# Pass one of a gated layer: the next tile's input products ahead of the output products, and four smaller moves

## The chip, the cores and the metric

One core of a Trainium2 chip runs the kernel. The metric is the device time of one execution in microseconds (us), the median of three runs. The engines are TensorE (PE, with PEld for its weight loads), VectorE (DVE), ScalarE (ACT), GpSimd (POOL) and SyncE (SP), which issues nearly all DMAs.

## The reference

Banded local attention and global attention (4 batches, 8 heads, 512 local and 32 global tokens each, 2176 tokens in all) give `x` with 512 features. `x` goes through two layers:

```
gated:     y = (sigmoid(x @ w_gate) * (x @ w_val)) @ w_out          # 512 -> 1536 -> 512
rational:  h = y @ w_in;   out = (P(h) / Q(h)) @ w_out2             # 512 -> 2048 -> 512, P and Q polynomials
```

The weights come as 64-bit floats and the result has to keep more precision than one 32-bit product gives.

## The kernel before

**Precision.** Each weight block is loaded raw and *converted* on the chip into a high and a low part in the matmul's 32-bit format (names ending in gv, in, out: the gate/value weights, the rational layer's first weights, and either layer's output weights). One conversion is a chain over three engines: two ACT operations (L566, L567), three on DVE (L574 to L576), an addition on POOL (L583), a high part on ACT (L605), a low part on POOL (L613), for some blocks further sums (combine: DVE L631, L634, L636, POOL L632, L643, ACT L642), and a store through SP (L597, from tiles named `st..` to DRAM tensors named `k..`). A product of two split operands is three matmuls (high by high, low by high, high by low), so twelve for the 512 features of one 128x512 output.

**Tiles.** The tokens lie in five tiles, 0 to 3 of 512 tokens and GLOB (4) of 128. The inner features `f` of the gated layer are 12 blocks of 128, and go in pairs `f0`, `f0+1`.

**Pass one** (the loop at L919 to L959) does tiles 0, 1 and GLOB for six pairs, f0 = 0, 2, .., 10. Its pieces:

- `first(f, i)`: 12 matmuls into `pg`, 12 into `pv` (L713 to L715), then the gate: sigmoid on ACT (L751), product on DVE (L752), high part on ACT (L759, `gh`), low part on DVE (L764, `gl`).
- `first_glob(f0)`: the same for GLOB with the operands turned; it ends with the gate product `t_glob` on DVE (L752).
- `turn(f0, t)`: PE transposes `t_glob` (L789, tile `pt`), then the split `gh_glob` (ACT L759) and `gl_glob` (DVE L764).
- `second_glob(f0, gg)`: six matmuls with `gh_glob` and `gl_glob` (L797 to L799), added to `gacc` on DVE (L806).
- halves (`second`, made by `pair_of`): 12 matmuls of output products each (L831 to L833), two additions to `gacc` on DVE (L845). A pair's two halves for one tile are kept in `pending` and placed later; in the last pair the sums are also split for DRAM (L848, L849), and `parks` holds such splits.

The order of an iteration before the change is: first(f0, 0), the two halves of tile 1 from the pair before, first(f0+1, 0), first_glob, the two halves of tile 0, turn, first(f0, 1), first(f0+1, 1), second_glob. Between the pieces `spot` lets `Pace` issue conversion steps, so that their instructions stand in the engines' queues among the others.

**Pass two** does tiles 2 and 3 for the other pairs by a Strassen scheme (`strassen`, L972, called for f = 2 to 11), in which sums `w`, `u`, `s` of PSUM results (L994) stand between products, with a list `fill` of halves placed between them, and `pace = Pace(actions, 143.0)` spreads the remaining conversions. `back(i)` (L964) asks tile i's results back from DRAM, eight SP DMAs (L969, L970); `rest()` (L1111) places the last halves.

**The rational layer** (`rational`, L1119) follows a table of operations per 128x512 unit. On ACT it makes `u`, `v` and `t1` (L1152, L1155, L1163), on POOL a product (L1159) and the low part `rgl` (L1213), on PE the output products (L1242 to L1244). `new` (L1136) takes the buffers: `t1` from the pool `rest`, which lies where the gated layer's closed pool was, with the stage tiles `st..` of the last conversions.

All engines run their instructions in program order, and SP its DMAs; nothing is reordered at run time. PSUM gives three banks to `ps1` (`pg`, `pv`) and five to `ps2`.

Of the kernel before, what the change touches and what calls it, by code (L numbers as in the profile page):

```python
# [8 lines left out]
F32 = mybir.dt.float32  # L9
# [699 lines left out]
def layer(nc, ps, wp, net, f, i, mh, ml):  # L709

    for k in range(4):
        wh, wl = wp.block(net, f, i, k)
        nc.tensor.matmul(ps, wh, mh[:, k], start=k == 0, stop=False)  # L713
        nc.tensor.matmul(ps, wh, ml[:, k], start=False, stop=False)  # L714
        nc.tensor.matmul(ps, wl, mh[:, k], start=False, stop=k == 3)  # L715
# [20 lines left out]
def gated(nc, pools, only, xpool, dram, wp, ident, xh, xl):  # L736
    G = G1
    NF = FF // 128
    L = 2.72
# [8 lines left out]
    def gate(pg, pv, name):  # L748

        t = pools.t.tile([128, 512], F32, tag="u", name=f"t{name}")[:, 0 : pg.shape[1]]  # L750
        nc.scalar.activation(t, pg, AF.Sigmoid)  # L751
        nc.vector.tensor_tensor(t, pv, t, ALU.mult)  # L752
        return t
# [12 lines left out]
    def split(t, name):  # L766
        g = high(t, name)
        low(t, g)
        return g

    def first(f, i):
        pg = pools.ps1.tile([128, 512], F32, tag="p1", name=f"pg{f}_{i}")
        pv = pools.ps1.tile([128, 512], F32, tag="p1", name=f"pv{f}_{i}")
        layer(nc, pg, wp, 1, f, "gate", xh[i], xl[i])
        layer(nc, pv, wp, 1, f, "val", xh[i], xl[i])
        return split(gate(pg, pv, f"{f}_{i}"), f"{f}_{i}")
# [43 lines left out]
    parks = []  # L820
# [52 lines left out]
    def ztile(name):  # L873
        return only.tile([128, 512], F32, tag="z", name=name, bufs=5)
# [11 lines left out]
    def less(dst, x, y, eng):  # L886

        for d, a, b in zip(dst, x, y):
            eng.tensor_tensor(d, a, b, ALU.subtract)
        eng.tensor_tensor(dst[0], dst[0], dst[1], ALU.add)  # L890

    def at(rc, k):
        return [t[:, k] for t in part[rc]]
# [18 lines left out]
    def c3(k):  # L912
        held["d", k], held["e", k] = ztile(f"zd{k}"), ztile(f"ze{k}")
        less((held["d", k], held["e", k]), at((1, 1), k), at((0, 1), k), nc.gpsimd)
# [4 lines left out]
    for p, f0 in enumerate(range(0, NF, G)):  # L919
        pace = Pace(wp.plan[p], 34.0)  # L920
        extra = {}
        if f0 + G == NF:
            load = lambda: wp.allow(1)
            extra = {0: [load], 1: [load], 2: [lambda: c1(0)], 3: [load], 4: [load, lambda: c2(0)], 5: [load, lambda: c4(0)],
                     6: [load], 7: [lambda: c3(0)] + [lambda: parks.pop(0)()] * 2, 8: [lambda: parks.pop(0)()] * 2}
        spots = iter(range(9))

        def spot(dt):
            pace.advance(dt)
            for step in extra.get(next(spots), []):  # L930
                step()

        gs = [first(f0, 0)]
        if p == 0:
            for step, j in wp.urgent[6:]:
                step(j)
        spot(2 * L)
        for half in pending or [lambda: None] * 2:
            half()
            spot(L if pending else 0)  # L940
        gs.append(first(f0 + 1, 0))
        pending = pair_of(f0, 0, gs)
        spot(2 * L)
        t = first_glob(f0)
        spot(3)
        for half in pending:
            half()
            spot(L)
        gg = turn(f0, t)
        gs = [first(f0, 1)]  # L950
        spot(2 * L)
        gs.append(first(f0 + 1, 1))
        second_glob(f0, gg)
        pending = pair_of(f0, 1, gs)
        for g in range(G):
            for h in range(2):
                wp.release((1, f0 + g, "gv", h))
        spot(0)
        pace.finish()  # L959
# [3 lines left out]
    actions = list(wp.plan[-1])  # L963
    def back(i):  # L964
        yh[i] = xpool.tile([128, 4, 512], F32R, tag=f"xh{i}", name=f"yh{i}")
        yl[i] = xpool.tile([128, 4, 512], F32R, tag=f"xl{i}", name=f"yl{i}")
        for m in range(4):
            t = wp.kept[9, i, "y", m]
            nc.sync.dma_start(yh[i][:, m].bitcast(F32), t[:, 0:512])  # L969
            nc.sync.dma_start(yl[i][:, m].bitcast(F32), t[:, 512:1024])  # L970

    def strassen(f, fill, before, gs):  # L972
        x = {(r, c): (xh[2 + c][:, 2 * r : 2 * r + 2], xl[2 + c][:, 2 * r : 2 * r + 2]) for r in range(2) for c in range(2)}
        def product(ps, key, moving, start):
            t = wp.have[1, f, key, 0]
            mh, ml = moving
            for k in range(2):
                w, v = slice(k * 128, k * 128 + 128), slice(256 + k * 128, 384 + k * 128)
                nc.tensor.matmul(ps, t[:, w], mh[:, k], start=start and k == 0, stop=False, skip_group_check=True)
                nc.tensor.matmul(ps, t[:, w], ml[:, k], start=False, stop=False, skip_group_check=True)  # L980
                nc.tensor.matmul(ps, t[:, v], mh[:, k], start=False, stop=k == 1, skip_group_check=True)

        def done(key):
            wp.release((1, f, key, 0))
            wp.pump(len(wp.loads))

        def bank(name):
            return pools.ps1.tile([128, 512], F32, tag="p1", name=f"{name}{f}")

        def tile(name):  # L990
            return only.tile([128, 512], F32, tag="z", name=f"{name}{f}", bufs=5)

        def add(out, ps, t):
            nc.vector.tensor_tensor(out, ps, t, ALU.add)  # L994

        def late(n):
            if before:
                before[n]()

        a, b, c = bank("pa"), bank("pb"), bank("pc")  # L1000
        product(a, "g0", x[0, 0], True)
        s1 = tile("s")
        nc.scalar.copy(s1, a)
        late(0)
        product(b, "s2", turned[1], True)
        done("g0")
        u2 = tile("u")
        add(u2, b, s1)
        late(1)
        product(c, "s1", turned[0], True)  # L1010
        late(2)
        if f == NF - 1:
            back(0)
        product(a, "g1", x[1, 0], False)
        done("s1")
        t0 = pools.t.tile([128, 512], F32, tag="u", name=f"t{f}_2")
        nc.scalar.activation(t0, a, AF.Sigmoid)
        late(3)
        pace.advance(2 * L)
        for half in fill[0:1]:  # L1020
            half()
            pace.advance(L)
        product(b, "s3", turned[2], False)
        u3 = tile("w")
        add(u3, b, s1)
        add(u3, c, u3)
        pace.advance(L / 2)
        for half in fill[1:2]:
            half()
            pace.advance(L)  # L1030
        product(b, "v1", turned[3], False)
        if f == NF - 1:
            back(1)
        done("s3")
        add(s1, b, s1)
        product(c, "s4", x[1, 1], False)
        done("s4")
        add(u2, c, u2)
        pace.advance(L)
        g = {}  # L1040

        def l0():
            nc.gpsimd.tensor_tensor(t0, s1, t0, ALU.mult)
            nc.scalar.activation(u2, u2, AF.Sigmoid)

        def l1():
            gs[0].append(g0 := high(t0, f"{f}_2"))
            g[0] = g0
            nc.gpsimd.tensor_tensor(u2, u3, u2, ALU.mult)

        def l2():
            low(t0, g[0])

        def l3():
            gs[1].append(g1 := high(u2, f"{f}_3"))
            low(u2, g1, nc.gpsimd)

        return [l0, l1, l2, l3]
# [5 lines left out]
    gs = [first(0, 2)]  # L1064
# [17 lines left out]
    gs = [first(0, 3)]  # L1082
# [13 lines left out]
        for h in range(2):  # L1096
            wp.release((1, f, "gv", h))
    wp.allow(len(wp.loads))
    pace = Pace(actions, 143.0)
    queue, tail = pair_of(0, 3, gs), []  # L1100
    for f0 in range(G, NF, G):
        sets, per = ([], []), len(queue) // G
        for f in range(f0, f0 + G):
            tail = strassen(f, queue[0:per], tail, sets)
            queue = queue[per:]
        queue = pair_of(f0, 2, sets[0]) + pair_of(f0, 3, sets[1])
# [4 lines left out]
    def rest():  # L1111
        for _ in range(2):
            queue.pop(0)()
        wp.pump(len(wp.loads))

    return yh, yl, rest
# [2 lines left out]
def rational(nc, pools, rest, wp, ident, xh, xl, before, co, out):  # L1119
    G = G2  # L1120
    NF = FF2 // 128
# [12 lines left out]
    st = [dict() for _ in units]  # L1134

    def new(u, name):  # L1136
        pool = {"u": pools.t, "v": wp.early}.get(name, rest)
        t = st[u][name] = pool.tile([128, 512], F32, tag=name, name=f"{name}{u}", bufs=3)
        return t

    def first(u):

        fs, i = units[u]
        ps = st[u]["h"] = pools.ps1.tile([128, 512], F32, tag="p1", name=f"rp{u}")
        if i == GLOB:
            turned_layer(nc, ps, wp, 2, fs[0], xh[i], xl[i])
        else:
            layer(nc, ps, wp, 2, fs[0], "in", xh[i], xl[i])
# [124 lines left out]
    for n in range(len(units) + 8):  # L1273
        for name, ahead, *args in PLAN2:
            u = n + ahead
# [117 lines left out]
```

## Time and profile before

| | |
|---|---|
| three runs | 956.99, 956.1, 956.0 us; median 956.1 |
| profiled execution | 957.4 us, span 955.6 us, granted clock 0.982 |
| busy share of the span | PE 95%, PEld 79%, DVE 79%, ACT 61%, POOL 60% |
| chain that ended last | PE 69%, POOL 9%, DVE 9%, issue 5%, DMA 4%, ACT 2% |
| attention | 0 to 125 us |
| pass one | 143 to 368 us |
| pass two | 401 to 552 us |
| rational layer | 555 us to the end |

A timeline row gives the start in us from the span's start, the duration in us, engine, line, operation and tiles, and in brackets the engine's idle time just before with what ended it. A matmul's duration there is its passage through the array: the next one starts 0.22 to 0.23 us later. A count (x4) joins equal instructions that follow one another.

### The profile page before, as it was taken

Reading aid. Unit: us, or ns where it says so; the run is one execution under the profiler, and the core shown is the slowest. Engines: PE = TensorE matmul, PEld = TensorE weight load, DVE = VectorE, ACT = ScalarE, POOL = GpSimd, SP = SyncE. Lnnn points to the kernel's source line nnn. Section 1 sums busy time; section 2 is a strip of 40 time slices with the busy share of each in tenths; the row PEclk is TensorE's granted clock in tenths of the full one; section 3 lists DMA queues with packets and bytes.
Section 4 is the critical chain, followed back from the end, with each engine's and each line's share of the span. In section 5 each row is a group of like instructions: output and inputs, shape, how many; then the busy total and the mean of one; then the engine's idle time right before and its main releaser. Section 6 shows DMA issues by size and latency. Waiting matters only on the chain.

```text
span 955.6 us, 13762 instructions
## 1 busy us (share of the span) xinstructions
PE 910.9 (95%) x4666; PEld 750.5 (79%) x4666; DVE 753.0 (79%) x1355; ACT 580.9 (61%) x1161; POOL 572.5 (60%) x470
## 2 busy tenths in 40 slices
PE   8989999898989899989999977999999999999998
PEld 6768888687867778868888856888888888888886
DVE  6988885887878777866866738977788899888887
ACT  6978963554545444343344436777776778777773
POOL 4765865666666755444666635544465667566564
PEclk9999999899999999999999998999999999999999
DMA  9865264666667677688888971003200310020112
GB/s 303 242 200 146 79 244 176 238 242 229 246 212 253 218 276 266 234 281 291 293 296 282 339 273 45 1 1 105 72 1 1 110 67 1 1 89 1 45 55 88
DMA packets 60805, 156.24 MB, mean 163 GB/s; under 512 B 7104, under 2 KB 9152, under 8 KB 60736
## 3 DMA queue, kind: packets, MB, share of 16 engines
q1 hardware_dynamic: 60640, 155.24, 46.9%
q8 instruction: 37, 0.61, 0.3%
q14 instruction: 32, 0.26, 0.1%
q10 hardware_dynamic: 96, 0.13, 0.1%
HBM read 103.17 MB, written 52.17 MB: 163 GB/s over the span
## 4 chain that ended last, share of the span: by engine, by line
PE 69%; POOL 9%; DVE 9%; issue 5%; DMA 4%; ACT 2%; SPq 1%; POOLq 0%; ACTq 0%; DVEq 0%
PE rp L1244 6%; PE rp L1242 6%; PE rp L1243 6%; PE rp L713 6%; PE rp L714 6%; PE rp L715 6%; PE pair L261 2%; PE p L833 2%; PE p L832 2%; PE p L831 2%; DMA qn<-in_q_l 2%; PE bank L380 1%; PE pg L713 1%; PE pg L714 1%; PE pg L715 1%
## 5 line engine op out<-in xcount | busy, mean ns | idle before, releaser
L1159 POOL TENSOR_TENSOR v<-v,u 128x512 f32<-128x512 f32 x68 | 90.8, 1336 | 119.3 <-ACT v L1155 119.3
L1213 POOL TENSOR_TENSOR rgl<-t,rgh 128x512 fp32r<-128x512 f32 x64 | 89.8, 1404 | 40.9 <-POOL v L1159 19.2
L1167 DVE TENSOR_TENSOR t<-rp,t 128x512 f32<-128x512 f32 x68 | 46.8, 688 | 53.6 <-ACT t L1163 52.5
L295 POOL TENSOR_TENSOR p<-p,r 128x448 f32<-128x448 f32 x64 | 58.6, 940 | 36.8 <-DVE r L290 23.7
L1152 ACT ACTIVATE u<-rp 128x512 f32<-128x512 f32 x68 | 40.5, 595 | 63.9 <-PE rp L715 60.3
L1188 DVE SCALAR_TENSOR_TENSOR v<-v,u 128x512 f32<-128x512 f32 x68 | 74.9, 1101 | 0.0
L1192 DVE SCALAR_TENSOR_TENSOR t<-t,co,v 128x512 f32<-128x512 f32 x68 | 72.9, 1072 | 2.4
L280 ACT ACTIVATE p<-p,mx 128x224 f32<-128x224 f32 x128 | 60.4, 485 | 7.6 <-DVE mx L272 7.6
L845 DVE TENSOR_TENSOR gacc<-p,gacc 128x512 f32<-128x512 f32 x80 | 51.3, 681 | 13.8 <-PE p L833 13.8
L1184 DVE SCALAR_TENSOR_TENSOR v<-v,u 128x512 f32<-128x512 f32 x68 | 59.1, 870 | 1.1 <-ACT u L1180 1.1
L759 ACT CAST gh<-t 128x512 fp32r<-128x512 f32 x38 | 23.6, 620 | 58.9 <-DVE t L752 51.5
L1163 ACT ACTIVATE t<-rp,co 128x512 f32<-128x512 f32 x68 | 51.8, 761 | 10.1 <-DMA k215out<-st215out 9.6
L1155 ACT ACTIVATE v<-u,co 128x512 f32<-128x512 f32 x68 | 55.6, 817 | 2.3
L764 DVE TENSOR_TENSOR gl<-t,gh 128x512 fp32r<-128x512 f32 x38 | 34.9, 917 | 26.2 <-ACT gh L759 26.2
L1176 ACT ACTIVATE u<-v,co 128x512 f32<-128x512 f32 x68 | 49.2, 724 | 6.0 <-POOL v L1159 6.0
L1171 DVE SCALAR_TENSOR_TENSOR t<-t,co,rp 128x512 f32<-128x512 f32 x68 | 50.2, 739 | 0.0
L1180 ACT ACTIVATE u<-u,co 128x512 f32<-128x512 f32 x68 | 48.5, 713 | 2.3 <-DVE t L1167 2.2
L1201 ACT CAST rgh<-t 128x512 fp32r<-128x512 f32 x64 | 39.1, 611 | 15.4 <-DVE t L1192 15.4
L272 DVE CUSTOM_DVE_ANT_0 p<-pair,masks 128x224 f32<-128x224 f32 x128 | 42.2, 384 | 7.0 <-DMA masks<-in_masks 6.4
L1267 POOL TENSOR_TENSOR racc<-ev,racc 128x512 f32<-128x512 f32 x22 | 37.9, 1742 | 0.0
L261 PE MATMUL pair<-kn,qn 64*128 64x224 f32 x256 | 30.2, 368 | 1.7 <-ACT pgn L319 1.2
L362 PE MATMUL bank<-ident,p 128*128 128x128 f32 x128 | 26.6, 291 | 1.3 <-POOL p L295 1.3
(1388 smaller groups left out, 3199.1 us busy)
## 6 DMA issues: line engine op xcount, KB each, us to landing
raw1gv<-in_w_gate_val SPq DMA_DIRECT2D x24, 512.0 KB, 4.0
raw2in<-in_w_in SPq DMA_DIRECT2D x16, 512.0 KB, 4.4
raw2out<-in_w_out SPq DMA_DIRECT2D x16, 512.0 KB, 3.7
kn<-in_k_l SPq DMA_DIRECT2D x15, 448.0 KB, 5.4
raw1out<-in_w_out SPq DMA_DIRECT2D x12, 512.0 KB, 3.6
vn<-in_v_l SPq DMA_DIRECT2D x16, 256.0 KB, 3.9
out<-racc SPq DMA_DIRECT2D x16, 256.0 KB, 2.0
qn<-in_q_l SPq DMA_DIRECT2D x15, 256.0 KB, 4.7
```

The costliest lines, as they stand in the source:

```text
L280: nc.scalar.activation(p, p, AF.Exp, bias=s["mx", half][:, n : n + 1], scale=-1.0, accum_out=s["sm", half][:, n, 0:1])
L295: nc.gpsimd.tensor_tensor(p, p, r, ALU.mult)
L713: nc.tensor.matmul(ps, wh, mh[:, k], start=k == 0, stop=False)
L714: nc.tensor.matmul(ps, wh, ml[:, k], start=False, stop=False)
L715: nc.tensor.matmul(ps, wl, mh[:, k], start=False, stop=k == 3)
L1159: nc.gpsimd.tensor_tensor(s["v"], s["v"], s["u"], ALU.mult)
L1184: nc.vector.scalar_tensor_tensor(s["v"], s["v"], Q_CONST, s["u"], ALU.add, ALU.mult)
L1188: nc.vector.scalar_tensor_tensor(s["v"], s["v"], 2.0, s["u"], ALU.subtract, ALU.mult)
L1192: nc.vector.scalar_tensor_tensor(s["t1"], s["t1"], a0, s["v"], ALU.add, ALU.mult)
L1213: nc.gpsimd.tensor_tensor(s["gl"], s["t1"], s["gh"].bitcast(F32), ALU.subtract)
L1242: nc.tensor.matmul(ps, gh[:, w], wh, start=k == 0, stop=False)
L1243: nc.tensor.matmul(ps, gh[:, w], wl, start=False, stop=False)
```

## The change

Five edits: (1) in pass one `first(f0, 1)` comes ahead of the two halves of tile 0, so that `turn` stands after the halves and one `first` instead of two lies between `turn` and `second_glob`; in the last pair one of four parked splits moves to an earlier spot. (2) In `strassen` a fill list that holds a single half has it placed at the second of two places instead of the first. (3) `back(1)` is issued after the last halves and no longer within the last Strassen step. (4) `Pace` of pass two gets 132 instead of 143. (5) The rational layer's `t1` uses the pool `wp.early` (tag `q`, three buffers), which the conversions' magnitude tiles used.

```diff
@@ -922,7 +922,8 @@
         if f0 + G == NF:
             load = lambda: wp.allow(1)
             extra = {0: [load], 1: [load], 2: [lambda: c1(0)], 3: [load], 4: [load, lambda: c2(0)], 5: [load, lambda: c4(0)],
-                     6: [load], 7: [lambda: c3(0)] + [lambda: parks.pop(0)()] * 2, 8: [lambda: parks.pop(0)()] * 2}
+                     6: [load, lambda: parks.pop(0)()], 7: [lambda: c3(0)] + [lambda: parks.pop(0)()] * 2,
+                     8: [lambda: parks.pop(0)()]}
         spots = iter(range(9))
 
         def spot(dt):
@@ -943,12 +944,12 @@
         spot(2 * L)
         t = first_glob(f0)
         spot(3)
+        gs = [first(f0, 1)]
+        spot(2 * L)
         for half in pending:
             half()
             spot(L)
         gg = turn(f0, t)
-        gs = [first(f0, 1)]
-        spot(2 * L)
         gs.append(first(f0 + 1, 1))
         second_glob(f0, gg)
         pending = pair_of(f0, 1, gs)
@@ -1017,7 +1018,7 @@
         nc.scalar.activation(t0, a, AF.Sigmoid)
         late(3)
         pace.advance(2 * L)
-        for half in fill[0:1]:
+        for half in fill[:-1]:
             half()
             pace.advance(L)
         product(b, "s3", turned[2], False)
@@ -1025,12 +1026,10 @@
         add(u3, b, s1)
         add(u3, c, u3)
         pace.advance(L / 2)
-        for half in fill[1:2]:
+        for half in fill[-1:]:
             half()
             pace.advance(L)
         product(b, "v1", turned[3], False)
-        if f == NF - 1:
-            back(1)
         done("s3")
         add(s1, b, s1)
         product(c, "s4", x[1, 1], False)
@@ -1096,7 +1095,7 @@
         for h in range(2):
             wp.release((1, f, "gv", h))
     wp.allow(len(wp.loads))
-    pace = Pace(actions, 143.0)
+    pace = Pace(actions, 132.0)
     queue, tail = pair_of(0, 3, gs), []
     for f0 in range(G, NF, G):
         sets, per = ([], []), len(queue) // G
@@ -1111,6 +1110,8 @@
     def rest():
         for _ in range(2):
             queue.pop(0)()
+        if not queue:
+            back(1)
         wp.pump(len(wp.loads))
 
     return yh, yl, rest
@@ -1134,8 +1135,8 @@
     st = [dict() for _ in units]
 
     def new(u, name):
-        pool = {"u": pools.t, "v": wp.early}.get(name, rest)
-        t = st[u][name] = pool.tile([128, 512], F32, tag=name, name=f"{name}{u}", bufs=3)
+        pool = pools.t if name == "u" else wp.early
+        t = st[u][name] = pool.tile([128, 512], F32, tag={"t1": "q"}.get(name, name), name=f"{name}{u}", bufs=3)
         return t
 
     def first(u):
```

Lines of the changed kernel are one higher from L926 on. Three places show the new order.

First, DVE in pass one, from the first conversion to the split behind it, in the iteration f0 = 4 (v17gv and v20in are conversions, p_0 are halves of tile 0, t_1, pv_1 and gl_1 belong to first(f, 1)). Before:

```order
L845 TENSOR_TENSOR gacc_1923<-p_0_0_2715,gacc_1923 128x512
L845 TENSOR_TENSOR gacc_1923<-p_0_1_2716,gacc_1923 128x512
L845 TENSOR_TENSOR gacc_1923<-p_0_2_2740,gacc_1923 128x512
L845 TENSOR_TENSOR gacc_1923<-p_0_3_2741,gacc_1923 128x512
L574 TENSOR_SCALAR v20in_2705<-v20in_2705 128x512
L575 TENSOR_SCALAR v20in_2705<-v20in_2705 128x512
L576 SCALAR_TENSOR_TENSOR v20in_2705<-raw2in_2601,v20in_2705 128x512
L764 TENSOR_TENSOR gl_glob<-pt_2769,gh_glob 128x256
L752 TENSOR_TENSOR t_1_2802<-pv_1_2777,t_1_2802 128x512
L764 TENSOR_TENSOR gl_1_2806<-t_1_2802,gh_1_2805 128x512
L631 TENSOR_TENSOR v17gv_2642<-v17gv_2578,v17gv_2642 128x256
```

With the change:

```order
L576 SCALAR_TENSOR_TENSOR v20in_2705<-raw2in_2601,v20in_2705 128x512
L845 TENSOR_TENSOR gacc_1981<-p_0_0_2770,gacc_1981 128x512
L845 TENSOR_TENSOR gacc_1981<-p_0_1_2771,gacc_1981 128x512
L631 TENSOR_TENSOR v17gv_2642<-v17gv_2578,v17gv_2642 128x256
L634 TENSOR_TENSOR v17gv_2578<-v17gv_2642,v17gv_2578 128x256
L636 TENSOR_TENSOR v17gv_2642<-v17gv_2642,v17gv_2578 128x256
L845 TENSOR_TENSOR gacc_1981<-p_0_2_2808,gacc_1981 128x512
L845 TENSOR_TENSOR gacc_1981<-p_0_3_2809,gacc_1981 128x512
L574 TENSOR_SCALAR v20in_2753<-v20in_2753 128x512
L575 TENSOR_SCALAR v20in_2753<-v20in_2753 128x512
L576 SCALAR_TENSOR_TENSOR v20in_2753<-raw2in_2649,v20in_2753 128x512
L764 TENSOR_TENSOR gl_glob<-pt_2832,gh_glob 128x256
```

The split `gl_glob` stood behind four additions and one conversion; now it stands also behind the combine of v17gv (L631 to L636) and a second conversion, and, ahead of these rows, behind one gate product and its split (L752, L764) that used to follow it.

Second, SP at the end of pass two (k91y is tile 1 in DRAM, w22out to w24in are weights loaded for the rational layer, st215out is a stage tile). Before:

```order
L970 DMA yl_5701<-k91y_4200 128x512
L969 DMA yh_5700<-k91y_4245 128x512
L970 DMA yl_5701<-k91y_4245 128x512
L662 DMA w22out_62_5710<-k22out_3679 128x1024
L662 DMA w23out_63_5719<-k23out_3694 128x1024
L662 DMA w24in_64_5721<-k24in_3896 128x1024
L662 DMA w24in_65_5723<-k24in_3974 128x1024
L597 DMA k215out_5729<-st215out_5726 128x1024
```

With the change:

```order
L662 DMA w21out_61_5642<-k21out_3295 128x1024
L597 DMA k214out_5651<-st214out_5590 128x1024
L597 DMA k215out_5656<-st215out_5653 128x1024
L662 DMA w22out_62_5705<-k22out_3679 128x1024
L662 DMA w23out_63_5714<-k23out_3694 128x1024
L662 DMA w24in_64_5716<-k24in_3913 128x1024
L662 DMA w24in_65_5718<-k24in_3949 128x1024
L970 DMA yh_5901<-k91y_4131 128x512
L971 DMA yl_5902<-k91y_4131 128x512
```

The store of st215out and the weight loads stood behind tile 1's eight loads, and now stand ahead of them.

Third, DVE in `strassen` at f = 3 (p_3_2 and p_3_3 are the lone half's results, w a Strassen sum that a product waits for). Before:

```order
L994 TENSOR_TENSOR u_4475<-pb_4454,s_4462 128x512
L764 TENSOR_TENSOR gl_2_4478<-t_2_4381,gh_2_4477 128x512
L574 TENSOR_SCALAR v26out_4424<-v26out_4424 128x512
L575 TENSOR_SCALAR v26out_4424<-v26out_4424 128x512
L576 SCALAR_TENSOR_TENSOR v26out_4424<-raw2out_3983,v26out_4424 128x512
L843 COPY gacc_4407<-p_3_2_4517 128x512
L843 COPY gacc_4407<-p_3_3_4518 128x512
L994 TENSOR_TENSOR w_4542<-pb_4454,s_4462 128x512
L994 TENSOR_TENSOR w_4542<-pc_4455,w_4542 128x512
```

With the change:

```order
L995 TENSOR_TENSOR u_4477<-pb_4456,s_4464 128x512
L764 TENSOR_TENSOR gl_2_4480<-t_2_4381,gh_2_4479 128x512
L574 TENSOR_SCALAR v26out_4424<-v26out_4424 128x512
L575 TENSOR_SCALAR v26out_4424<-v26out_4424 128x512
L576 SCALAR_TENSOR_TENSOR v26out_4424<-raw2out_3981,v26out_4424 128x512
L995 TENSOR_TENSOR w_4524<-pb_4456,s_4464 128x512
L995 TENSOR_TENSOR w_4524<-pc_4457,w_4524 128x512
L843 COPY gacc_4421<-p_3_2_4529 128x512
L843 COPY gacc_4421<-p_3_3_4530 128x512
```

The two copies of the lone half's results stood ahead of `w` and now stand behind it.

## Rows read from the trace of the kernel before

**Rows 1.** Waits of PE, whole span: us in total, times, longest.

```profile
PE pt L789 <- DVE t_glob L752: 12.1, 4, 3.1
PE p L831 <- DVE gacc L845: 7.1, 1, 7.1
PE rp L1244 <- POOL rgl L1213: 4.4, 1, 4.4
PE pb L979 <- DVE w L994: 3.3, 2, 2.5
PE p L833 <- POOL w111out L613: 0.9, 1, 0.9
```

**Rows 2.** Busy time in an iteration of pass one: stretch, length, engines, clock, DMA.

```profile
core 0: us, PE busy (x) PEld busy (x) DVE busy (x) ACT busy (x) POOL busy (x), PEclk, DMA share, GB/s
229.50:272.30 42.80, 39.43 (x177) 32.19 (x177) 34.34 (x50) 21.05 (x39) 28.61 (x22) 0.96 0.68 234
```

**Rows 3.** Waits of DVE, 157 to 360 us: the one for PE.

```profile
DVE t L752 <- PE pv L715: 0.6, 1, 0.6
```

**Rows 4.** Timeline of DVE in iteration f0 = 2.

```profile
186.15 0.42 DVE L752 TENSOR_TENSOR t_glob<-pgv,t_glob 128x256 f32<-128x256 f32 x1
...
190.29 2.47 DVE L845 TENSOR_TENSOR gacc<-p,gacc 128x512 f32<-128x512 f32 x4
...
194.38 0.42 DVE L764 TENSOR_TENSOR gl_glob<-pt,gh_glob 128x256 fp32r<-128x256 f32 x1
...
197.55 0.41 DVE L631 TENSOR_TENSOR v15gv<-v15gv,v15gv 128x256 f32<-128x256 f32 x1
...
201.59 1.67 DVE L576 SCALAR_TENSOR_TENSOR v20in<-raw2in,v20in 128x512 uint32<-128x512 uint32 x1
...
208.68 0.69 DVE L752 TENSOR_TENSOR t<-pv,t 128x512 f32<-128x512 f32 x1 [0.82 <-ACT t L751]
```

**Rows 5.** Timeline of POOL there.

```profile
190.45 1.28 POOL L583 TENSOR_TENSOR v15gv<-v15gv,q15gv 128x512 uint32<-128x512 uint32 x1 [0.63 <-DVE v15gv L576]
...
195.79 1.29 POOL L613 TENSOR_TENSOR w15gv<-v15gv,w15gv 128x512 fp32r<-128x512 f32 x1
```

**Rows 6.** Timeline of PE there: second_glob's first matmul, and the next first's last.

```profile
200.53 0.39 PE L797 MATMUL p_glob<-w12out,gh_glob 128*128 128x512 f32 x1
...
207.11 0.39 PE L715 MATMUL pv<-xh,w14gv 128*128 128x512 f32 x1
```

**Rows 7.** Windows behind waits of PE, columns as in rows 2.

```profile
186.60:192.40 5.80, 5.77 (x15) 4.62 (x16) 5.73 (x8) 4.38 (x9) 4.80 (x4) 0.50 0.61 202
272.20:276.20 4.00, 3.94 (x18) 3.29 (x19) 3.93 (x6) 3.71 (x7) 2.97 (x3) 1.00 0.38 140
573.80:577.90 4.10, 4.09 (x10) 3.23 (x11) 3.02 (x4) 2.15 (x4) 1.53 (x2) 0.50 0.00 0
```

**Rows 8.** Timeline in the last pair, f0 = 10: first(10, 0) on PE, its gate product on DVE.

```profile
334.43 0.39 PE L715 MATMUL pv<-xh,w110gv 128*128 128x512 f32 x1
337.15 0.69 DVE L752 TENSOR_TENSOR t<-pv,t 128x512 f32<-128x512 f32 x1 [0.84 <-ACT t L751]
```

**Rows 9.** Timeline of DVE in strassen, f = 3.

```profile
425.00 1.27 DVE L843 COPY gacc<-p 128x512 f32<-128x512 f32 x2
426.19 0.67 DVE L994 TENSOR_TENSOR w<-pb,s 128x512 f32<-128x512 f32 x1
```

**Rows 10.** Timeline where the rational layer starts: ACT, SP, POOL.

```profile
557.89 0.82 ACT L1155 ACTIVATE v<-u,co 128x512 f32<-128x512 f32 x1
568.35 0.78 ACT L1163 ACTIVATE t<-rp,co 128x512 f32<-128x512 f32 x1 [9.64 <-DMA k215out<-st215out]
...
559.94 0.32 SPq L597 DMA_DIRECT2D k215out<-st215out  x1
...
558.79 1.29 POOL L1159 TENSOR_TENSOR v<-v,u 128x512 f32<-128x512 f32 x1 [1.57 <-ACT v L1155]
...
589.38 1.72 POOL L1213 TENSOR_TENSOR rgl<-t,rgh 128x512 fp32r<-128x512 f32 x1
```

## The prediction

> **What bounds the kernel now.** I read the waits of TensorE first, for the stalls that the edits could remove; then, for each, the timeline of the engine it waits for, because a stall of a 95% busy engine may still be another engine's period. [Rows 1] list PE's waits behind the attention. The largest belongs to pass one: four times the transposes wait for `t_glob`, 12.1 us in all. One reads from it that PE would gain 12.1 us if the turn came later. [Rows 2] and [rows 3] say otherwise. An iteration takes 42.80 us, in which PE is busy for 39.43 and DVE for 34.34; and over all of pass one DVE waits for PE's products 0.6 us only. So PE sits idle 3.4 us an iteration while nobody waits for it: the period is set by the conversions' chain through DVE, POOL and ACT, in which DVE executes its queue in order, and `t_glob`, a gate product, is late because it stands in that queue among conversion steps. A later turn then saves nothing by itself; what counts is whether something the DVE queue needs from PE becomes late.
>
> **Pass one, f0 = 2 to 8.** The work stays the same; 12 + 12 + 24 matmuls and the DVE steps that use them change places. Before, `gl_glob` ran at 194.38, 8.2 us after `t_glob` at 186.15 [rows 4], and PE needed it only at 200.53 [rows 6]. By the first pair of orders it now stands behind everything DVE did up to the second conversion v20in, whose last step ran from 201.59 for 1.67 us, to 203.26 [rows 4]. To lay it out: the same operations in the new order cannot end much earlier, because the combine (L631, 197.55 before) waits for POOL's low part, 195.79 plus 1.29 [rows 5], itself behind the addition of the first conversion. That conversion moves up to the gate product's place and ends some 0.8 later than before, L631 moves to 197.8, the two pairs of additions, half of 2.47 each, lie on either side of it, the second conversion's bits end at 204.0, and `gl_glob`, 0.42 long, at 204.4. PE meanwhile has done first(f0, 1), both halves, the turn and first(f0+1, 1) without a wait and would start `second_glob` at about 192.8. So the stall moves there and becomes longer, 11.6 us here and some 8 later on, where PE's lead is smaller. That alone is idle time of an engine which is ahead. It costs what it makes late: the next iteration's first(f0, 0), whose `pv` DVE wants at 208.68 [rows 4]. From the first matmul with `gl_glob` to the end of that `pv` are 28 matmuls. At the spacing in [rows 6], 30 matmuls from 200.53 to 207.11 or 0.227 each, that is 6.4 us, to which the last one's passage adds some 0.2 and the hand-over 0.1.
>
> The **clock** is the unknown in this. Behind the stall of 7.1 in the rational layer [rows 1] the stretch from 573.80 had clock 0.50, 1.2 GHz, with 10 matmuls in 4.10 us where 18 fit at 2.4 GHz [rows 7]: 8 matmuls lost, 1.8 us. A stall of 3.1 before 272.20 left the clock at 1.00 (cost 0), and a longer slow stretch, 186.60 to 192.40, ran 15 where 25 fit (10 lost, 2.4 us). I take 1.8, since the new stalls are nearest in length to the first row's; the ends are 0 and 2.4. The Trainium skill, "TensorE: Matmul & The Clock Gate", section "What's actually happening", puts the ramp's penalty below 1% of a typical kernel's span and advises against fitting it; by that alone no clock term would stand in the sum, which is case B below.
>
> So `pv` is there at 204.4 + 6.4 + 1.8 + 0.2 = 212.8, 4.1 later than wanted. Some 0.1 of it comes back, since two combine steps now meet a free POOL: **+4.0 us for each of four iterations, +16.0**. With `gl_glob` at 203.7 and no clock loss it is +1.5 less the part that the next conversion can fill, +0.9 at least; with 2.4 of clock and 1 us more of sharing between DVE and POOL, +5.5. f0 = 0 has fewer conversions in the queue, its `gl_glob` comes in time, and costs 0 (0 to +2).
>
> **Pass one, f0 = 10.** PE ends first(10, 0)'s `pv` at 334.43 + 0.39, and DVE takes it at 337.15 [rows 8]: a lead of 2.3 us. The late `second_glob` of f0 = 8 spends it: the +4.0 above are already counted, and what the lead had paid for behind it comes on top, +2.3. The wait for w111out, 0.9 [rows 1], is hidden by it: -0.9. This iteration's own `gl_glob` is late behind one more conversion and a split of the last pair on DVE: 2.0 of wait and half of the clock's 1.8, +2.9. Together **+4.3** (0 to +7). The parked split that moves earlier is one ACT operation and one subtraction, in cover of the same stall: 0.
>
> **Strassen.** At f = 3 the copies of the lone half, 1.27, stood just ahead of `w` [rows 9] and now stand behind it; PE's longest of two waits for `w`, 2.5 [rows 1], becomes 1.4: -1.1. f = 2 had the other, 0.8, which goes: -0.8. A shorter wait may leave the clock up: half of 1.8, -0.9. At f = 6 and 9 the faster pace puts a second conversion ahead of `w`, which has some lead: +0.3. Sum **-2.5** (-4 to -1). The pace of 132 issues the same steps earlier; where no `w` is behind them, PE covers them, and it costs 0.
>
> **The rational layer's start.** ACT's first `t1` at 568.35 waited 9.64 us for the store of st215out, as its buffer lay over that stage tile [rows 10]; SP issued that store at 559.94, behind tile 1's eight loads and four weight loads. The change takes away both, the buffer's place and SP's order (the second pair of orders). `t1` can then follow `v` at 557.89 + 0.82, and the quadratic step behind it waits for POOL until 558.79 + 1.29 = 560.08, so 0.7 of the gain is lost again: **-8.9** on the chain from 568.35 through POOL's low part at 589.38 [rows 10], to PE's stall of 4.4 for `rgl`. PE's stall of 7.1 for `gacc` before it [rows 1] is part of the same chain and goes; 4.4 stays. Bounds: -9.6 with everything shifted, and 0 if a conversion's `q` buffer or another stage store is as late; I take the first, since the conversions' tiles are all done before 557. Tile 1's loads come some 3 us later; its first product is over 100 matmuls behind 589, so the cover is some 24 us.
>
> **Sum:** +16.0 + 0 + 4.3 - 2.5 - 8.9 = +8.9. The profiled execution took 957.4, 1.3 above the median of 956.1; 966.3 there is **965.0** as a median. Adding the terms' probable errors (1 per iteration, 2 at f0 = 10, 1 in Strassen) gives 958 to 971 for this case by itself.
>
> **The rivals.**
>
> *A, faster: gl_glob is not late.* If `gl_glob` is ready 2.3 us earlier than I lay out, at 202 or so, and the clock stays up, `pv` meets DVE at 208.7 and pass one costs nothing. Then only -2.5 and -8.9 are left: 956.1 - 11.4 = 944.7, say 945. For it: that DVE is busy for only 34.34 of 42.80 us [rows 2], so its queue might close up. Against: its gaps are waits for POOL inside the conversions, which no reordering of the gate steps shortens. This is the case on the other side, and 4.1 us an iteration is the whole of its margin.
>
> *B, the clock does not fall.* By the row at 272.20 [rows 7] PE runs on at 2.4 GHz after a stall. Without 4 x 1.8 and the half of 1.8 at f0 = 10, and without Strassen's half of 1.8 that was to be won, the sum is 8.9 - 7.2 - 0.9 + 0.9 = +1.7, a median of 957.8: no change. Against it are the other two of these rows, after a longer stall and in a longer stretch.
>
> *C, PE is the bound after all.* Then all of the 12.1 us of `t_glob` waits go, with the slow stretches behind them, some 4 x 1.8, and the 11.4: about 926. Against it [rows 3].
>
> *D, the rational start does not move*, since another late store or load takes the place of st215out's: 965.0 + 8.9 = 974.
>
> *E, the pace's extra conversions stall Strassen* at f = 6 and 9, 1.5 and a slow stretch each, in place of the gain there: about 970.
>
> **How the numbers follow.** The forecast has 0.55, A 0.16, B 0.11, C 0.05, D 0.05, E 0.08. The range of 8 in 10 goes from A's time, 945, to 971, the upper end of the forecast, with E inside; C, D and half of A are left out. No change means within 0.2%, 1.9 us, about what a measurement of this kernel can tell. Faster: A, C and 0.05 from the lower ends of the forecast and B, 0.26. Same: half of B, 0.06. Slower: the rest, 0.68.
>
> **What would show it.** Right: PE's waits for `t_glob` gone, and in their place four or five of 8 to 12 us for `gl_glob` at `second_glob`; clock 0.50 behind them; new waits of DVE's gate product for `pv`, 3 to 4 us each; an iteration of some 46.8 us; ACT's wait for st215out gone, and the first output products of the rational layer some 9 us sooner after pass two. Wrong: an iteration still at 42.8 with no wait of DVE for `pv` (A or B, told apart by the clock), at 39.5 (C), or ACT's first `t1` still behind a DMA (D).

## The result, and the profile after

The changed kernel took 963.03 us (median of four runs, 961.38 to 964.1), the kernel before 956.55 in the same comparison: a ratio of 1.0063, 95% interval 1.0043 to 1.0084. It is slower. The forecast was 965.0, with 958 to 971 for its case and 945 to 971 for the whole. The profiled execution is the fastest of the four, 961.38 us with a span of 959.5 and a clock of 0.977; so between the two profiled executions lie 4.0 us, between the medians 6.5, and the stages below are compared in the traces. Even there an execution has its own share: pass one, behind an attention that no edit touches, begins between 123.2 and 125.8 us in the traces of this document.

PE's waits in the changed kernel, from 115 us on (us in total, times, longest), to be read beside [rows 1]:

```profile
PE p_glob L797 <- ACT gh_glob L759: 27.8, 4, 9.5
PE rp L1245 <- POOL rgl L1214: 4.9, 1, 4.9
PE p_glob L799 <- DVE gl_glob L764: 4.1, 5, 2.3
```

The waits for `t_glob`, for `w` and for `gacc` are gone. In their place stand waits at `second_glob`, four of 6 to 10 us and one of 2.3 at f0 = 10, 31.9 us together as against the 22.5 that went. The rest of the reading is whether anyone waits for PE; DVE's waits from 157 to 370 us answer to [rows 3]:

```profile
DVE t L752 <- PE pv L715: 13.9, 4, 4.3
```

That wait was 0.6 us and is now 13.9. The timeline of the iteration f0 = 2 shows how the one makes the other, PE first, then ACT and DVE, to be compared with [rows 4] and [rows 6]:

```profile
202.62 0.79 PE L797 MATMUL p_glob<-w12out,gh_glob 128*128 128x512 f32 x1 [9.53 <-ACT gh_glob L759]
203.21 0.63 PE L798 MATMUL p_glob<-w12out,gh_glob 128*128 128x512 f32 x1
204.31 0.79 PE L799 MATMUL p_glob<-w12out,gl_glob 128*128 128x512 f32 x1 [0.47 <-DVE gl_glob L764]
```

```profile
202.19 0.37 ACT L759 CAST gh_glob<-pt 128x256 fp32r<-128x256 f32 x1
202.46 0.60 ACT L751 ACTIVATE t<-pg 128x512 f32<-128x512 f32 x1
```

```profile
203.23 0.69 DVE L576 SCALAR_TENSOR_TENSOR v20in<-raw2in,v20in 128x512 uint32<-128x512 uint32 x1
203.84 0.42 DVE L764 TENSOR_TENSOR gl_glob<-pt,gh_glob 128x256 fp32r<-128x256 f32 x1
...
212.02 0.69 DVE L752 TENSOR_TENSOR t<-pv,t 128x512 f32<-128x512 f32 x1 [2.84 <-PE pv L715]
```

`gl_glob` ran from 203.84 to 204.26, after the second conversion, where 204.4 had been laid out; DVE took the next `pv` at 212.02 instead of 208.68 [rows 4], where 212.8 had been. `gh_glob` is nearly as late, in ACT's queue; the laying-out had looked at DVE alone. The clock behind the four stalls, columns as in [rows 2]:

```profile
202.62:206.18 3.56, 3.09 (x7) 1.99 (x7) 2.84 (x5) 1.06 (x2) 2.47 (x3) 0.50 1.01 328
248.36:251.91 3.55, 3.09 (x6) 1.99 (x7) 2.83 (x5) 1.06 (x2) 2.46 (x3) 0.50 1.00 319
295.05:298.61 3.56, 3.10 (x7) 1.99 (x8) 2.84 (x5) 1.06 (x2) 2.47 (x3) 0.50 1.05 332
342.29:345.83 3.54, 3.09 (x6) 1.99 (x7) 2.82 (x5) 1.06 (x2) 2.45 (x3) 0.50 1.02 326
```

Each of the four is followed by a stretch at 0.50, 1.2 GHz; the fifth, at f0 = 10, is not. From the spacing of PE's matmuls beyond 0.227 us the slow stretches took 1.8, 2.8, 3.3 and 1.9 us from PE.

By stage, from the first matmul of each in the two traces: pass one with the first pair of tiles 2 and 3, from 125.08 to 401.07 before and from 125.25 to 419.18 after, became 17.9 us longer (forecast +20.3). Pass two, to 552.27 and 565.03, became 5.4 shorter (forecast -2.5). The rational layer, to its product with w24out at 685.40 and 689.29, 8.9 shorter (forecast -8.9).

In Strassen, DVE at f = 3 of the changed kernel, beside [rows 9]:

```profile
436.77 0.43 DVE L575 TENSOR_SCALAR v26out<-v26out 128x512 uint32<-128x512 uint32 x1
437.23 0.69 DVE L576 SCALAR_TENSOR_TENSOR v26out<-raw2out,v26out 128x512 uint32<-128x512 uint32 x1
438.74 0.69 DVE L995 TENSOR_TENSOR w<-pb,s 128x512 f32<-128x512 f32 x1 [0.81 <-PE pb L982]
```

`w` no longer stands behind copies, and also waits for nothing but PE. The conversion ahead of it ran its long steps in 0.43 and 0.69 us, while POOL lay idle between these two:

```profile
434.56 1.30 POOL L1048 TENSOR_TENSOR u<-w,u 128x512 f32<-128x512 f32 x1 [0.49 <-ACT u L1043]
438.56 1.29 POOL L764 TENSOR_TENSOR gl<-u,gh 128x512 fp32r<-128x512 f32 x1 [2.71 <-ACT gh L759]
```

Before, the same steps were these, with POOL at work beside them:

```profile
421.97 1.40 DVE L575 TENSOR_SCALAR v26out<-v26out 128x512 uint32<-128x512 uint32 x1
423.41 1.66 DVE L576 SCALAR_TENSOR_TENSOR v26out<-raw2out,v26out 128x512 uint32<-128x512 uint32 x1
```

```profile
421.79 1.30 POOL L764 TENSOR_TENSOR gl<-u,gh 128x512 fp32r<-128x512 f32 x1 [0.74 <-DMA w15g<-k15g]
423.05 1.47 POOL L613 TENSOR_TENSOR st24out<-v24out,st24out 128x512 fp32r<-128x512 f32 x1
```

At the rational layer's start ACT, SP and POOL of the changed kernel answer to [rows 10]:

```profile
570.65 0.82 ACT L1156 ACTIVATE v<-u,co 128x512 f32<-128x512 f32 x1
571.37 0.76 ACT L1164 ACTIVATE t<-rp,co 128x512 f32<-128x512 f32 x1
572.87 0.72 ACT L1177 ACTIVATE u<-v,co 128x512 f32<-128x512 f32 x1 [0.74 <-POOL v L1160]
```

```profile
560.85 0.32 SPq L597 DMA_DIRECT2D k215out<-st215out  x1
```

```profile
559.39 1.31 POOL L613 TENSOR_TENSOR st215out<-v215out,st215out 128x512 fp32r<-128x512 f32 x1
```

`t1` follows `v` at once, and the next step waits 0.74 for POOL, as forecast. But POOL has also finished the last stage tile at 560.70, 4.3 us ahead of the layer's first matmul at 565.03. In the kernel before it finished at 552.63, just behind that matmul at 552.27:

```profile
551.34 1.29 POOL L613 TENSOR_TENSOR st215out<-v215out,st215out 128x512 fp32r<-128x512 f32 x1
```

So the faster pace may have had a part here that the prediction did not give it; its run alone, below, tells.

### The profile page after: what moved, and what is told of

The parts are those of the page before. It is cut to its first block, busy times and chain, and to the rows that moved or that the text cites. A ratio compares the mean times of both kernels' runs of the same rounds, so it can differ in the third digit from the quotient of the medians.

```text
span 959.5 us, 13769 instructions
## 1 busy us (share of the span) xinstructions
PE 907.8 (95%) x4666; PEld 749.0 (78%) x4666; DVE 753.1 (78%) x1355; ACT 581.4 (61%) x1161; POOL 572.1 (60%) x470
## 4 chain that ended last, share of the span: by engine, by line
PE 72%; DVE 13%; POOL 5%; DMA 4%; issue 3%; ACT 2%; SPq 1%; POOLq 0%; DVEq 0%; ACTq 0%
PE rp L1245 6%; PE rp L1243 6%; PE rp L1244 6%; PE rp L715 6%; PE rp L713 6%; PE rp L714 6%; PE p L833 2%; PE p L832 2%; PE p L831 2%; PE pair L261 2%; PE pg L713 2%; PE pg L714 2%; PE pg L715 1%; PE bank L380 1%; PE pv L715 1%
## 5 line engine op out<-in xcount | busy, mean ns | idle before, releaser
L764 DVE TENSOR_TENSOR gl<-t,gh 128x512 fp32r<-128x512 f32 x38 | 35.5, 934 | 27.2 <-ACT gh L759 27.2
L752 DVE TENSOR_TENSOR t<-pv,t 128x512 f32<-128x512 f32 x28 | 19.2, 685 | 25.8 <-PE pv L715 24.5
```

## The experiments

Eleven kernels ran, each beside the kernel before on the same chip, whose median there was 957.8 to 958.1 us. Ratios are to that.

**The reorder alone.** The kernel before with the first edit:

```diff
-        for half in pending:
-            half()
-            spot(L)
-        gg = turn(f0, t)
         gs = [first(f0, 1)]
         spot(2 * L)
+        for half in pending:
+            half()
+            spot(L)
+        gg = turn(f0, t)
```

> The kernel before with the first edit alone (first(f0, 1) ahead of the halves of tile 0, and the one park). Theory, the cost sits in pass one's new order and nowhere else: pass one becomes 17.9 us longer, as between the traces of before and after, the rational layer's start stays as before, so about 974 us; PE waits for gh_glob and gl_glob at second_glob four times, 6 to 9.5 us each. Rival, the loss in pass one comes from the changed kernel's other edits as well (a different pace of conversions, other buffers): less than half of it shows, 965 us or below.

978.35 us, ratio 1.0217 (1.0194 to 1.0239), 20.2 over before. Pass one is 20.6 longer in its trace, and PE's waits are those of the changed kernel:

```profile
PE p_glob L797 <- ACT gh_glob L759: 27.8, 4, 9.6
PE p L831 <- DVE gacc L845: 6.9, 1, 6.9
PE rp L1245 <- POOL rgl L1214: 4.7, 1, 4.7
PE p_glob L799 <- DVE gl_glob L764: 4.1, 5, 2.3
PE pb L980 <- DVE w L995: 3.3, 2, 2.5
```

The loss belongs to the first edit, and the stalls that the other edits remove are all still there. That pass one lost 20.6 us here and 17.9 in the changed kernel, by the same edit, lies in the clock at least in part: f0 = 10 has a slow stretch here (columns as in [rows 2]),

```profile
384.53:387.93 3.40, 3.40 (x10) 2.61 (x9) 2.72 (x4) 1.14 (x2) 1.66 (x2) 0.50 0.91 354
```

and none there. From the last `t_glob` to pass two it is 52.99 us here and 51.39 there.

**Everything but the reorder.**

```diff
-        gs = [first(f0, 1)]
-        spot(2 * L)
         for half in pending:
             half()
             spot(L)
         gg = turn(f0, t)
+        gs = [first(f0, 1)]
+        spot(2 * L)
```

> The changed kernel without its first edit: pass one as before, the other four edits kept. Theory: 956.5 less 5.4 in Strassen and less 8.9 at the rational layer's start, as the two traces differ there, 942.3 us, faster than both kernels. Rival, the gains in these stages depend on the later arrival from pass one (conversions that had longer to finish while PE stalled): 948 us or more.

944.06 us, ratio 0.9856 (0.9837 to 0.9875): 14.1 under before, as expected. PE's waits for `t_glob` are back at 12.1 us, and pass one takes 276.2 us as against 276.0 before. The two runs add up to the change: +20.2 and -14.1 are +6.1, and the changed kernel took 6.5 us more.

**The turn ahead of the halves.** The changed kernel with

```diff
         gs = [first(f0, 1)]
         spot(2 * L)
+        gg = turn(f0, t)
         for half in pending:
             half()
             spot(L)
-        gg = turn(f0, t)
```

> The changed kernel with the turn moved back to between first(f0, 1) and the two halves of tile 0, so that gh_glob and gl_glob stand in ACT's and DVE's queues ahead of the combine and of the second conversion. Theory, the queue place of the split is the whole cost: no wait of PE at second_glob, no wait for t_glob either, pass one as long as before because the conversions' chain sets its period, 942 to 945 us. Rival, the earlier place of first(f0, 1) costs by itself: 955 us or more. Rival, PE bounds pass one once all its stalls are gone: 930 us or less.

946.42 us, ratio 0.9885 (0.9866 to 0.9904). Of the 20.2 us all but 2.4 go with the queue place of one turn and its split. The expectation that PE would have no stall at all was wrong: it waits for `t_glob` as before, only longer,

```profile
PE pt L789 <- DVE t_glob L752: 17.3, 4, 4.8
```

and runs slow stretches at 0.50 behind it (186.90 to 191.80, 13 matmuls in 4.90 us). DVE waits for `pv` 0.7 us. So PE's stall grew by 5.2 us in four places from which DVE does not wait; what each iteration gained in length is 0.55 us, of which more below.

**Work in the place of the stall.** The changed kernel with, ahead of `second_glob`'s own matmuls,

```diff
+        for _ in range(24 if 0 < f0 < 10 else 0):
+            nc.tensor.matmul(ps, xh[GLOB][:, 0], wp.outer(1, f0)[0], start=True, stop=True)
```

> The changed kernel with 24 matmuls more ahead of second_glob for f0 = 2 to 8, whose result is overwritten: 5.4 us of PE's work in the place of the stall. Theory, the slow clock behind the stall is about half of the loss: the granted clock stays at 1.00 behind second_glob, the 9.8 us lost there in four iterations go, pass one's DVE waits for pv fall from 13.9 to about 4 us, and the time to 953 plus or minus 2 us although PE does more. Rival, the lateness is set by the queues alone and the clock only fills idle time: 963 us. Rival, the clock falls all the same and the extra matmuls add up: above 965 us.

957.03 us, ratio 0.9990 (0.9979 to 1.0002): better than the changed kernel's 1.0063, with 96 matmuls more. Pass one is 4.5 us shorter in the trace than in the changed kernel's. For f0 = 4, 6 and 8 the clock stays up:

```profile
247.69:251.24 3.55, 2.59 (x10) 1.85 (x11) 2.83 (x5) 1.06 (x2) 2.46 (x3) 1.00 1.03 335
292.52:296.07 3.55, 2.59 (x10) 1.85 (x11) 2.83 (x5) 1.06 (x2) 2.46 (x3) 1.00 1.00 337
337.34:340.89 3.55, 2.57 (x10) 1.81 (x11) 2.83 (x5) 1.06 (x2) 2.46 (x3) 1.00 1.04 331
200.20:207.30 7.10, 5.10 (x14) 3.76 (x15) 6.28 (x10) 3.85 (x8) 3.87 (x3) 0.76 0.84 295
```

At f0 = 2 (the last row) it doesn't; there PE waited 2.8 us for an addition to `gacc` ahead of the added work, and 1.1 and 1.0 us behind it for the two splits. DVE's waits for `pv` fell only to 11.9 us, and the gain in pass one is about half of the 9.8 us that the slow stretches took from PE: without the clock `pv` is still late, because 28 matmuls follow a late `gl_glob`. Both theories held in part.

**second_glob behind the next product.** The changed kernel with

```diff
         spot(2 * L)
+        for args in glob:
+            second_glob(*args)
         for half in pending or [lambda: None] * 2:
...
-        second_glob(f0, gg)
+        glob = [(f0, gg)]
+        if f0 + G == NF:
+            second_glob(f0, gg)
```

> The changed kernel with second_glob of each pair but the last placed behind the next pair's first(f0, 0); the turn and its late split stay where the change put them. Theory, a late gl_glob costs only because first(f0, 0) of the next pair stands behind the wait on PE: with that product ahead of the wait pv comes in time, DVE's waits for pv (13.9 us in the changed kernel) fall to under 2, and the time is 11 to 14 us under before although gh_glob and gl_glob are as late as in the changed kernel. Rival, the new order of DVE's own queue (the combine and two conversions ahead of the split) costs by itself: 0 to 5 us over before.

951.57 us, ratio 0.9936 (0.9918 to 0.9955): 6.3 under before, between the two expectations. DVE waits for `pv` 3.0 us, yet PE still stalls, at another place, and runs 8 to 11 matmuls at 0.50 behind each of the four:

```profile
PE pv L713 <- ACT t L751: 20.5, 4, 7.1
PE p_glob L799 <- DVE gl_glob L764: 2.3, 1, 2.3
```

The next `pv` needs the third bank of `ps1`, and that is free once the sigmoid of first(f0+1, 1) has read its `pg`, which stands in ACT's queue behind `gh_glob`. A second late reader was hidden behind the first.

From one `t_glob` on DVE to the next, and from the last to the start of pass two, in the traces (us):

| | f0=2 | 4 | 6 | 8 | 10 to pass two |
|---|---|---|---|---|---|
| before | 42.84 | 42.80 | 42.82 | 38.60 | 47.86 |
| turn ahead of the halves | 43.39 | 43.37 | 43.36 | 39.19 | 48.40 |
| second_glob later | 43.81 | 43.86 | 43.86 | 39.72 | 51.38 |
| work in the stall | 46.44 | 44.83 | 44.83 | 40.84 | 51.38 |
| the change | 45.68 | 46.68 | 47.24 | 41.81 | 51.39 |

The steps from row to row give an estimate of each cause for f0 = 4 to 8: 0.54 to 0.59 for the order of the gate steps, 0.5 for the late split, 1.0 to 1.1 for `pv` behind it, and 1.0 to 2.4 for the clock. It is an estimate, since each row is one execution and the second and third rows have slow stretches of their own. The clock's step is not the same in the next execution: with the same pass one, the slow stretches of the run of the reorder alone took 3.0, 1.8, 2.8 and 3.4 us from PE, where those of the changed kernel took 1.8, 2.8, 3.3 and 1.9.

**One edit at a time.** Each is an edit of the change made alone in the kernel before. The pool of `t1`:

```diff
-        pool = {"u": pools.t, "v": wp.early}.get(name, rest)
-        t = st[u][name] = pool.tile([128, 512], F32, tag=name, name=f"{name}{u}", bufs=3)
+        pool = pools.t if name == "u" else wp.early
+        t = st[u][name] = pool.tile([128, 512], F32, tag={"t1": "q"}.get(name, name), name=f"{name}{u}", bufs=3)
```

> The kernel before with the fifth edit alone (t1 in the pool of the conversions' magnitude tiles). Theory: the buffer's place is enough, ACT's wait of 9.6 us for st215out goes though SP's order is the old one: 8.9 us under before. Rival, tile 1's eight loads ahead of it on SP hold something else up: under 4 us of gain.

948.73 us, ratio 0.9907 (0.9881 to 0.9933), 8.9 under before; ACT's wait is gone. In the trace only 7.8 of it come at the rational layer's start. Strassen, which this edit doesn't touch, is 1.5 shorter: PE waits the same 2.48 us for `w`, but the clock stays up behind it. Here are the wait and the 3.4 us from it, first before, then in this run (columns as in [rows 2]):

```profile
426.92:430.32 3.40, 3.40 (x10) 2.74 (x11) 1.37 (x2) 1.23 (x2) 1.25 (x2) 0.65 0.92 315
425.83:429.23 3.40, 3.40 (x15) 2.78 (x16) 1.67 (x3) 1.21 (x2) 1.67 (x2) 1.00 0.93 316
```

Tile 1 asked back later:

```diff
-        if f == NF - 1:
-            back(1)
...
+        if not queue:
+            back(1)
```

> The kernel before with the third edit alone (tile 1 asked back after the last halves). Theory: the store of st215out is issued ahead of tile 1's loads, about 553 instead of 559.9 us, so that t1 comes some 7 us sooner: 5 to 8 us under before, and the two edits share one gain. Rival, the store itself is slow whenever it starts: under 3 us of gain.

952.70 us, ratio 0.9945 (0.9925 to 0.9964), 5.3 under before (4.2 at the rational layer's start in the trace). The store went out at 554.59, and `t1` still waited 5.5 us for a DMA:

```profile
564.11 0.78 ACT L1163 ACTIVATE t<-rp,co 128x512 f32<-128x512 f32 x1 [5.52 <-DMA yh<-k91y]
```

The lone half:

```diff
-        for half in fill[0:1]:
+        for half in fill[:-1]:
...
-        for half in fill[1:2]:
+        for half in fill[-1:]:
```

> The kernel before with the second edit alone (a lone half at the second place of a Strassen step). Theory: both of PE's waits for w (3.3 us) go with the slow clock behind the longer one, all of the 5.4 us that Strassen gained: 5.4 under before. Rival, the faster pace has part in it: 2 to 4 under before.

953.75 us, ratio 0.9960 (0.9948 to 0.9972), 3.8 under before: the rival. One wait of PE for `w` is left, 1.3 us, behind a conversion still at 1.40 and 1.67 us, and no slow stretch behind it. Strassen is 3.9 shorter in the trace. The pace:

```diff
-    pace = Pace(actions, 143.0)
+    pace = Pace(actions, 132.0)
```

> The kernel before with the fourth edit alone (a pace of 132 instead of 143 in pass two). Theory: the pace moves POOL's part of the conversions away from the conversion that stands ahead of w at f = 3, which then runs its two long DVE steps in 0.43 and 0.69 instead of 1.40 and 1.66 us; alone that takes up to 1.9 us from PE's wait of 2.5, and 1 to 3.5 us from the whole, with the clock. Rival, as the prediction had it, the pace is worth nothing: within 0.7 us of before.

946.34 us, ratio 0.9879 (0.9863 to 0.9896): 11.6 under before, far outside both expectations. Strassen is 3.0 shorter in the trace, and 8.1 come at the rational layer's start. POOL has finished the last stage tile 4.3 us ahead of the layer's first matmul at 549.06, and SP issues its store ahead of tile 1's loads by itself:

```profile
543.42 1.30 POOL L613 TENSOR_TENSOR st215out<-v215out,st215out 128x512 fp32r<-128x512 f32 x1
```

```profile
544.81 0.32 SPq L597 DMA_DIRECT2D k215out<-st215out  x1
547.90 0.32 SPq L969 DMA_DIRECT2D yh<-k91y  x1
```

Two combinations followed, of the edits shown: the lone half with the pace, and these two with the pool of `t1`.

> The kernel before with the second and fourth edits together. Theory: no wait of PE for w is left in pass two, 5.4 us under before, some 1.5 more than the second edit alone gave in its trace. Rival, the rest of the gain in the changed kernel came from its later start of pass two: 4 us under before or less.

942.37 us, ratio 0.9837 (0.9822 to 0.9852), 15.5 under before, the lowest time of all. Strassen is 5.3 shorter, as the theory had it, and the 8.9 at the rational layer's start, which it had left out, come on top. PE's waits between 400 and 600 us:

```profile
PE rp L1244 <- POOL rgl L1213: 4.9, 1, 4.9
```

> The kernel before with the second, fourth and fifth edits, tile 1 asked back at its old place. Theory: with t1 in the other pool nobody waits for st215out, and the third edit adds nothing to it: 13 to 14.5 us under before, as the run without the first edit. Rival, tile 1's loads ahead of the last stores and weight loads cost something of their own: 12 us under or less.

943.51 us, ratio 0.9844 (0.9828 to 0.9860), 14.3 under before, as expected. Neither the third nor the fifth edit adds anything that can be measured to the pace and the lone half. With both of them, the version without the reorder reached 0.9856, and the intervals of the three overlap.

## Why the prediction was right, and where it was not

**The period of pass one** is not PE's: right. In the kernel before, a slow stretch stands behind the wait at f0 = 2 and none at f0 = 6 [rows 7], and the two iterations last 42.84 and 42.82 us; and with the turn ahead of the halves PE waits 5.2 us more for `t_glob` while DVE's waits for `pv` are 0.7 us as against 0.6. The reorder costs its 20.2 us by what it makes late.

**The late split** was laid out within 0.2 us, and `pv` within 0.8. The wait was expected on `gl_glob`; the profile names `gh_glob` for 27.8 of 31.9 us, since ACT's queue is as late. PE could have used `gh_glob` sooner for only two matmuls ahead of `gl_glob`, so this changes the stall's name, not its end. What the working lacked was the PSUM bank behind it, which the fifth experiment showed. In the changed kernel this second late reader is hidden, so it changes no term of the sum.

**+16.0 for f0 = 2 to 8** measured +14.35 by the table, and the 0 for f0 = 0 measured 0.06. Without the clock the forecast was 2.2 an iteration, and the run with work in the stall has 2.0 to 2.2 for f0 = 4 to 8. The clock's 1.8 measured 1.9, 2.4 and 1.0 there. The case in which the clock doesn't fall is ruled out by the four rows at 0.50. How long a stall lasts does not settle it in these traces, as the choice of 1.8 by the nearest length had it: behind waits of 2.5 to 3.1 us the clock fell in some places and stayed in others, and behind one and the same wait for `w` it did either. The Trainium skill, "TensorE: Matmul & The Clock Gate", section "What's actually happening", puts the ramp below 1% of a typical span. The traces are near it: the 4.5 us that came back with the clock are 0.5%, and the 9.8 that the four slow stretches took from PE 1.0%. But the whole effect of the change is 0.63%, so the clock could not be left out of the sum.

**+4.3 at f0 = 10** measured 3.5. The step that failed within it is the 2.3 for PE's lost lead: the interval ahead of it grew by 3.2, no more than its neighbours. The iteration's own late `gl_glob` cost some 3.0 and the order of the gate steps 0.5, which the run with the turn ahead of the halves has as well (48.40 as against 47.86); that run has the moved split too, so the 0 for it holds. Half of a slow stretch had been counted, and none came; in the run of the reorder alone one came and cost 1.6.

**-2.5 in Strassen** measured -5.4. The failed step is that the pace "costs 0", covered by PE. As laid out the lone half took the first wait and 1.2 of the second (run alone: 1.3 of 2.5 left). The faster pace moved POOL's steps away from the conversion ahead of `w`, whose two steps then took 1.12 instead of 3.06 us, and the last wait went. The slow stretch, counted by half, went whole, with either edit alone. Alone the lone half gives 3.9 in its trace, where 2.8 had been laid out, and the pace 3.0, where it was to cost 0.3.

**-8.9 at the rational start** measured -8.9, and the size is right for a reason that was only one of three. In this stage the pool of `t1` alone gives 7.8 by its trace, the pace alone, which the prediction had at nothing, 8.1, and the order on SP alone 4.2. They remove one wait and share one gain. That the changed kernel's own share can't be given to any one of them follows.

**The sum** of the stages is +3.7 in the traces as against a forecast of +8.9. The errors of pass one (2.4) and Strassen (2.9) have the same sign: both stages came out shorter than worked out. The profiled executions, 4.0 apart, bear this out; the medians are 6.5 apart, nearer to the forecast, and that part of the agreement is spread between runs. By the medians the reorder alone costs 20.2, where +20.3 was forecast, and the other four edits bring 14.1, where 11.4 was; so by the medians pass one is as forecast, and the miss is in Strassen. One price of the rivals does not add up: the case in which the pace stalls Strassen, 1.5 and 1.8 at two places in place of -2.5, is about 974 and not 970, above the range that was to hold it. It did not come: the changed kernel has no wait for `w`.

Open is why the order of the gate steps costs 0.55 an iteration when no engine waits for PE. DVE's waits for POOL's low parts in pass one rose from 13.0 to 17.4 us, by four new ones of 1.1, one in each iteration from f0 = 2 to 8; that fits, but no run took it apart.

## What to carry to other kernels

A stall of the busiest engine is worth what waits behind it: read first whether anyone waits for that engine, and then where a moved step comes to stand in every in-order queue that it passes. A small step at the end of a long queue can make late what a whole iteration needs, and the slow clock behind the stall can add half as much or as much again. Edits that remove the same wait are to be tried one at a time: here a single number for the pace did what two others were made for, and two of the five edits make a kernel 2.2% faster than all five do.

## What was not expected of the hardware

The same DVE steps of a conversion took 1.40 and 1.66 us with POOL busy and 0.43 and 0.69 with POOL idle, a factor of 2.4 to 3.3, and which of the two a conversion gets depends on the pace that places POOL's work. The Trainium skill, "GPSIMD Engine Reference", section "Specifications", has GpSimd share its SBUF interfaces with VectorE, with contention for DVE instructions with two SBUF inputs or in a 2-port performance mode; the rows agree for L576, which has two inputs, while L575 has one and no row shows its mode.

The traces say more of what happens. Of the 68 steps of L575 in the kernel before, the 42 with POOL idle beside them took 0.43 us; the other 26 began while a POOL instruction ran, and every one of them ended 0.28 to 0.29 us after that instruction. For L576 the same is 47 steps of 0.69 us and 18 that ended 0.55 us after POOL's; three more, beside which POOL began later than they did, took 0.69. So such a step is not slower throughout: it gets no further until the POOL instruction ahead of it has ended.

24 further matmuls an iteration made the kernel faster, 957.0 instead of the 964 or so that the changed kernel's ratio gives on that chip, of which the clock at 1.00 in three of four places explains 4.5 us by the trace of pass one. The two profiled executions are 5.9 us apart; the other 1.5 lie in attention, which the added matmuls don't touch.
